# A new written order for 1363 jobs of an attention and two-MoE kernel: the order table, the engine table and one number of the planner

## The chip, the cores and the metric

The kernel runs on one core of one Trainium2 chip. The metric is the device time of one execution in microseconds (us); a version is timed by the median of its runs.

## What is computed

Three stages follow one another, all in FP32. Attention has 2 batches of 8 heads, 768 positions and a head width of 64; each query sees keys less than 16 positions away, and in addition one key for each of the 24 blocks of 32 (the maximum of the block's keys; its value is their mean). The first MoE mixes along the positions, the second convolves along them. Shortened, with shapes as comments:

```python
k_sum = k.reshape(B, H, nb, 32, D).max(axis=3); v_sum = v.reshape(B, H, nb, 32, D).mean(axis=3)
scores_l = where(abs(i - j) < 16, scale * q @ k.T, -1e9)
scores_s = scale * q @ k_sum.T + log(32)
a = softmax(concat([scores_l, scores_s]))            # 768 + 24 columns
x = a @ concat([v, v_sum])                           # then (2, 768, 512)
h = relu(x @ w_in); u, v = h[..., :512], h[..., 512:]
v_s = w_spatial @ layernorm(v) + b_spatial           # 768 x 768 over the positions
x = (u * v_s) @ w_out                                # (2, 768, 512)
h = relu(x @ w_in2)                                  # (2, 768, 1024)
out = (h * sigmoid(conv3(h, conv_w))) @ w_out2       # conv3 over the positions
```

## The kernel before

**Attention.** Two heads of a batch stand together on 128 partitions and are called a pair, n = 0 to 7. A pair has two groups of six blocks of 64 queries; group i is half i mod 2 of pair i div 2, 16 groups in all. For one group TensorE (PE) makes the scores (lines 461, 468 and 474; 96 window keys and 24 block keys for each block), VectorE (DVE) takes the row maximum (478), ScalarE (ACT) does six exps with their sums (482), DVE sums and inverts (485, 488), GpSimd (POOL) or DVE normalises (491). Then PE transposes the weights, three blocks at a time in two parts (495, "first" and "second" transposes), into the one buffer `pt`; each part is copied out by ACT or DVE (517). PE multiplies them with the values (501), and the result is split into a rounded part `xh` (522) and a rest `xl` (523). The scores have two buffers, `s_80` for even groups and `s_81` for odd ones; query and key tiles alternate between even and odd pairs. The block keys come from `keys` (lines 391 to 406), the block means of the values from `means`, on PE (417) for pairs 0 and 2, by a reduction on DVE (424) and a transpose (427) for the others.

**Matrix products.** An FP32 product is three matmuls of rounded parts, high × high, low × high and high × low (lines 309 to 311, 256 or 512 columns each). The weights are split into such parts on ACT, POOL and DVE (`convert`; `sub_lo`, line 278, makes the rest). The first products of MoE 1 are mixed into the attention; then come its mix along the positions, the product of w_out and w_in2, and MoE 2 with its convolution (688), sigmoid (691), gate (694) and output.

**What sets the order.** Nothing is scheduled while the kernel runs. Each piece of work is recorded as a job with the engines that may do it and a planned time, 1363 jobs. `ORDER` names the jobs in the order in which they are issued, two characters each (a number to base 64), and `PICK` names for each job with a choice which of its engines takes it. An engine executes its jobs in this order, each waiting for what it needs. All loads go through SP's one queue in the same order, and a load waits there until its tile is free. The planned times have one effect only: where the plan sees PE idle for 0.5 us or more ahead of the dense products, it puts filler matmuls there, whose result nobody reads (line 740):

```python
if self.fill and gap >= 0.5:
    n = int((gap - 0.1) / 0.22)
    out.append((free.get(e, 0.0), k, e, 0.22 * n, lambda n=n, f=self.fill[1]: f(n)))
```

A load's planned time is its size over `RATE` = 276 KB per us, after which it is taken to land.

Of the kernel before, what the change touches and what calls it, by code (L numbers as in the profile page):

```python
# [20 lines left out]
B, H, S, D = 2, 8, 768, 64  # L21
# [27 lines left out]
STEPV = 4.5  # L49
SIGNS = "ABCDEFGHIJKLMNOPQRSTUVWXYZabcdefghijklmnopqrstuvwxyz0123456789+-"  # L50
ORDER = (
    "AGACAAABADAEAFAgAiASATAjAkAUAVAWAhAXAHAqALBYAYArAsAMBZAIAZAaBbBaBcA3A4A5AbAcAdANBiAJAlAtAuBjBECTCRAOBvAvAwAeBFCUCSA6CVA7"
    "BwA8AKB8DJAmAnBkBlAxAyAzAoBmApBnBGCbBHB9DKA9A0CcBxDIDHDLByBzB0A+A-BAA1A2BRB+BSCoCpB-APCdBdBoBpBBCeCfCgBCBqBrCqDRB1B2BDBe"
    "BfBgAfC1EgEhDSDTCDBhDwCECrCsB3B4DeDfDgBIBKBLAQBsBtChBuBJCWARB5B6C3ETC2CiCjCkEeCXCYCZCaCtCuBMBTBNBOCFBUCGBVCHCIB7EnDUDVBW"
    "CJClCmCvCwCxDrEoDWDXDhCACnCyDiDMCzC0EfE0FNBPBQDjBXDYFODZEpDNDODPDsDxDyDaDkFMEqErEsEiE1DlCBDbDcDdDQDmFPDtDACKEUC5C7C6DnC8"
    "C9EtC+C-CCFBDoDpE2DqCMCLCNCOEuDBDCDDDEDFFVFvFiEjFjE3E4EkDzDuD0D6D7D8D9F8F7DvD1CPD+DGE5CQEvEwD2F9F6D3D4FWFkEEE6EFEGFwD5Gm"
    "EXD-EAEBECFXEYEHFCGDE7EZEaFFEbGQC4FzFGGlElExFYEcEmFZEVFDFHFIFJFaEDGRE8EdF0EyEIE9EJEKELEMGEFQEzGnFKEOEPEQFbERF1F2FLF3F4Gk"
    "GSGTGUF5E+E-FAG6GFGtGuENHHHIFcFdEWGdGeESHRFRFSHSHJGfGgFTGhGiHTFlFmFeF+FfFgGjHUGvGwGxHKFnFoHVHlGGGHHmFpFqHWFhFUGVG7HnHoGI"
    "HLHMFrGJGKG8G9FsHpHbFtHcHdG+FuG-HXGLF-GAHeGMIiGWIDHqFEGBGNJ8J5FyFxGXGYIEH5HfHgGOGPGyGCGZGzIyG0GaHvHwGoHNHOHxHhHiGbGcHjHk"
    "HPHQG1G2GpHyHzH0IzIaLNHAHBIjHYGqGsH6GrHCLUHDINIFHZHaIbH7IcH8H1I3H9G3G4ItG5IIIOHEIJHFISIkH+HrH-HGITIGIULOH2LPIKILH3IAIBH4"  # L60
    "HsICHtHuIuIdIPInIHIlIQIRI9IMIvIVI+IWJbJcJdJeLbI-IeImJvJAIfIgI4IoIXIpI6I5IYIZIqI7I8IrIsIwIxLQLRJBJCJHJRJIJJJKJLJMJwJSJTJU"
    "JVIhJfJgJxJyI0I1KRKvI2JNJOJlJhJWJPJiLWKwJmKxJnJQJzJXJYKHKIKJKKKLJDJEJZKMJoJ9KbKcJjJaKlKdKeKfKgLDKmJ+LEJkKNJFJGJ0JpJqK5LS"
    "J1KOJrJsJ2JtLTKPJuLVJ3KQJ4KhKiLXLYKSK6KjKTKkLdJ-LZLaLcLeLiLfLFKUKVKWKAKBKCLGLHLIK7K8LpKnKoKXLgKyKpM-LJLhLKKYNnMrNAKDKELk"
    "LjLwLlLmMsNBKqKFKGKrLnKsLrKZMtLoKtLqL3K9KaK+K-LALBNJNCNDNKNLLsLtKzLyLuLvNENdNMNNM1M2M3M4K0NeNOLLLxL+KuM5LzL0LMNFNfNgNhMu"
    "MhMvMiMjMkMlMmK1NTMwL1L2L4NGLCL5MFNHL6K2L7K3K4MxL8L9MnMoL-MAMBMCMMNoNUNVOvM6MpM7MqMDMEM8MHMGMTMIMJNPM9M+NQOpO7MKMLO8NiNp"
    "OqNqO1O2MNNIMOMaMPMQNjMRMyOrO3NWNrMzNsNtOsOtMSMUNRO9O4O5M0MVNxNXMWMXMYNuNYO+OwPNPOPTOxPBNZO6PHOuPIMZOyPPPCPJMcMbNkMdMePD"
    "MfMgNSOzNlO-NzJ6NmNyO0N0NvN1PEPFPrPUPVPsN2N3PAN4N6PKN5N7N8PtPQPRPuPwPxNaN9N+NbPSN-OAOBOCPyONPGPePfPgPLODOEPMPhPZQPJ7PjPv"
    "NcPWPzOFP0P2P1NwQCOGPXPaPbP3OIOHOUPiPYOJOKPcQDPdPkPlOLOMQEQFQGQHOOPmPnOPP9QQP+P-OQORPoQmOSQAQBQhPpOTOVP4QnQUOWQVOXOYQIOZ"
    "QJQoQ4PqQWQKQzP5P6QXQYQRQSQTQaQbObOiQ5QLP7RFQMQNQcRGQiQ6QjP8Q0OdQOQ1QpQdQqQrQkQlQsQZRHOaRIQ7RKQ8OcQeRLQtQ2QuQfQ3QvOeOfQw"
    "Q+Q-RJOgQxRARXRcRdRYRMReRfOhRZQ9OjQgRNROOkRBRQOlOmRCQyOnRDRRRSOoR2RuRpSaSbRaRbRgRiRTRERjRkRlSDRqSER3SFSGR4SNSOR5SPRURmRV"  # L70
    "RnRWSHSIRrRsRtRvSJRoSKSLR6SQSRR7R8RPRhRwSSRxRySTScR9R+RzR0SMSdSUSeR-SfR1SpSgSAShSkSVSBSlSiSCSmSWSjTASnSXSxSoSySqTXSzSYSr"
    "S0S1SZS2SsS3S4StS7S5SuS8S6TuS9SvS+SwTIS-TJTBTKTCTLTMTDTNTETOTPTFTSTQT7TTTGTRTUTHTVTfTWTgTYThTZTiTjTaTkTbTlTmTcTpTnTqTdTo"
    "TrTeTsT2TtT3TvT4TwT5UDTxT6UET8UFTyT9UGUHTzUIT+T0UJT1UKT-UNULUAUOUMUPUBUQUCURUSUTUUUXUVUYUWUZUaUbUcUdUeUhUfUiUgUjUkUlUmUn"
    "UoUrUpUsUqUtUuUvUwUxUyU1UzU2U0U3U4U5U6U7U8U-U9VAVBU+VCVDVEVFVGVJVHVKVIVLVMVNVOVPVQVRVS"
)
# [7 lines left out]
class Plan:  # L83
# [118 lines left out]
def block_kernel(ctx, tc, q_in, k_in, vwin, v_in, w_in, w_spT, b_sp, w_outT, w_in2, conv, w_out2, out):  # L202
    nc = tc.nc
    PE, DVE, ACT, POOL, SP = nc.tensor, nc.vector, nc.scalar, nc.gpsimd, nc.sync
# [162 lines left out]
    def load_values(n):
        j, r = n % 2, STEP * NG * n
# [524 lines left out]
```

## Time and profile before

| | before |
|---|---|
| median of 3 runs | 333.48 us (333.2 to 333.6) |
| profiled execution, its own time | 332.87 us |
| span of the profile | 331.1 us |
| PE busy | 326.1 us, 98% of the span |
| DVE, ACT, POOL busy | 234.8, 188.9, 69.4 us |
| share of PE in the chain that ended last | 93% |

The span runs from the first to the last instruction of the profiled execution; the execution's own time has in addition what lies around the span. Busy times are sums over an engine's instructions. PE's weight loads run beside its matmuls and are listed as an engine of their own.

### The profile page before, as it was taken

The numbers are of one execution on the slowest core, as the hardware profiler recorded it, in microseconds if no ns is written. First come the engines' busy times: TensorE is split into PE (matmuls) and PEld (weight loads), VectorE is DVE, ScalarE is ACT, GpSimd is POOL, SyncE is SP. The second block draws the span as 40 slices with busy tenths as digits, with TensorE's granted clock in tenths as the row PEclk, the third lists the DMA queues.
The fourth block names the chain that finished last, engine by engine and source line by source line (L and its number), as shares of the span: only waits on it lengthen the run. The fifth ranks groups of instructions, "written<-read, shape, count | busy, mean of one in ns | idle before, by whom it ended". The sixth has DMA issues, their size and how long they took to land.

```text
span 331.1 us, 6200 instructions
## 1 busy us (share of the span) xinstructions
PE 326.1 (98%) x2391; PEld 269.3 (81%) x2391; DVE 234.8 (71%) x433; ACT 188.9 (57%) x463; POOL 69.4 (21%) x91
## 2 busy tenths in 40 slices
PE   8999999999999999999999999999999999999996
PEld 3677888878888889888988888888888888888886
DVE  5899899876663378678989878898996976470000
ACT  3999888866545443334444355978776865461111
POOL 5696953475040213000111101000000000000000
PEclk9999999999999999999999999999999999999999
DMA  7999649724244300112334423240000010000101
GB/s 220 317 302 318 195 154 319 204 62 122 68 157 157 98 0 0 65 63 90 103 127 129 127 63 127 65 127 1 2 1 1 30 65 32 32 32 34 63 32 65
DMA packets 13325, 34.50 MB, mean 104 GB/s; under 512 B 1648, under 2 KB 3952, under 8 KB 13296
## 3 DMA queue, kind: packets, MB, share of 16 engines
q1 hardware_dynamic: 13296, 34.11, 32.8%
q8 instruction: 19, 0.31, 0.4%
q14 instruction: 10, 0.08, 0.1%
HBM read 30.96 MB, written 3.15 MB: 103 GB/s over the span
## 4 chain that ended last, share of the span: by engine, by line
PE 93%; DMA 3%; ACT 2%; SPq 1%; issue 0%; ACTq 0%
PE late L309 12%; PE late L310 12%; PE late L311 12%; PE mm L309 9%; PE mm L310 9%; PE mm L311 9%; PE xp L501 4%; PE pt L495 3%; PE xp L309 3%; PE xp L310 3%; PE xp L311 3%; PE pt L309 3%; PE pt L310 3%; PE pt L311 3%; DMA a<-vwin 2%; PE s L474 2%
## 5 line engine op out<-in xcount | busy, mean ns | idle before, releaser
L688 DVE SCALAR_TENSOR_TENSOR v<-v,conv_t 128x767 f32<-128x767 f32 x32 | 32.5, 1015 | 9.8 <-ACT v L685 9.5
L482 ACT ACTIVATE a<-s,a 128x120 f32<-128x120 f32 x96 | 33.4, 391 | 0.7 <-DVE a L478 0.6
L278 POOL TENSOR_TENSOR w<-a,w 128x256 fp32r<-128x256 f32 (+1 forms) x15 | 15.2, 1013 | 53.4 <-ACT w L284 52.9
L293 ACT ACTIVATE a<-a 128x512 f32<-128x512 f32 (+1 forms) x25 | 16.3, 650 | 12.4 <-POOL w L278 4.2
L482 ACT ACTIVATION_READ_ACCUMULATOR a<-s,a 128x1 f32 x96 | 22.7, 237 | 0.0
L298 DVE SCALAR_TENSOR_TENSOR a<-a,a 128x512 uint32<-128x512 uint32 (+1 forms) x32 | 19.9, 624 | 3.8 <-ACT a L293 1.4
L491 POOL TENSOR_TENSOR a<-a,a 128x720 f32<-128x720 f32 x15 | 20.8, 1392 | 3.9 <-DVE a L488 3.8
L300 DVE SCALAR_TENSOR_TENSOR a<-a,a 128x512 uint32<-128x512 uint32 (+1 forms) x32 | 19.9, 624 | 0.9
L691 ACT ACTIVATE v<-v 128x768 f32<-128x768 f32 x16 | 13.5, 846 | 9.6 <-DVE v L688 9.6
L309 PE MATMUL late<-xh,a 128*128 128x512 f32 x48 | 18.7, 389 | 0.0
L310 PE MATMUL late<-xl,a 128*128 128x512 f32 x48 | 18.7, 389 | 0.0
L311 PE MATMUL late<-xh,a 128*128 128x512 f32 x48 | 18.7, 389 | 0.0
L694 DVE TENSOR_TENSOR v<-v 128x768 f32<-128x768 f32 x16 | 15.3, 956 | 3.7 <-ACT v L691 3.4
L495 PE MATMUL pt<-ident,a 128*120 128x128 f32 x96 | 16.6, 281 | 0.4 <-ACT a L517 0.4
L729 ACT COPY tmp<-late 128x512 f32<-128x512 f32 x7 | 4.1, 583 | 20.3 <-PE late L311 20.3
L478 DVE TENSOR_REDUCE a<-s 128x6 f32<-128x720 f32 x16 | 14.3, 897 | 1.8 <-PE s L474 1.8
L278 DVE TENSOR_TENSOR a<-tmp,a 128x512 fp32r<-128x512 f32 (+1 forms) x10 | 8.0, 830 | 10.5 <-ACT a L284 10.4
L501 PEld LDWEIGHTS xp<-a,a 120*64 120x64 f32 x384 | 12.5, 137 | 3.4 <-issue 1.9
L685 ACT ACTIVATE v<-v,conv_t 128x768 f32<-128x768 f32 x16 | 15.0, 939 | 0.4
L501 PE MATMUL xp<-a,a 120*64 120x64 f32 x384 | 14.7, 226 | 0.0
L309 PE MATMUL mm<-xh,w 128*128 128x256 f32 (+1 forms) x40 | 14.5, 362 | 0.0
L495 PEld LDWEIGHTS pt<-ident,a 128*120 128x120 f32 x96 | 10.6, 137 | 4.7 <-issue 1.3
(331 smaller groups left out, 1018.4 us busy)
## 6 DMA issues: line engine op xcount, KB each, us to landing
a<-w_in SPq DMA_DIRECT2D x12, 512.0 KB, 3.8
a<-w_out SPq DMA_DIRECT2D x8, 512.0 KB, 3.7
out<-tmp SPq DMA_DIRECT2D x11, 256.0 KB, 2.0
a<-vwin SPq DMA_DIRECT2D x8, 288.0 KB, 6.1
a<-v_in SPq DMA_DIRECT2D x6, 384.0 KB, 6.3
a<-vwin SPq DMA_DIRECT2D x4, 576.0 KB, 7.1
tmp<-w_spT SPq DMA_DIRECT2D x6, 384.0 KB, 3.4
a<-w_in SPq DMA_DIRECT2D x8, 256.0 KB, 5.7
```

The lines of the kernel that those rows point to most:

```text
L278: eng.tensor_tensor(out=lo.r(), in0=src.f(), in1=hi.f(), op=ALU.subtract)
L293: mul = {"ACT": (0.2 + n / 1080, lambda: ACT.mul(fu.f(), half(1).bitcast(F32), 2.0 ** -112)), "POOL": (0.18 + n / 1050, lambda: POOL.tenso ...
L298: add({"DVE": (0.16 + n / 960, lambda: DVE.scalar_tensor_tensor(out=last.u(), in0=fu.u(), scalar=0x80000000, in1=last.u(), op0=ALU.bitwise ...
L300: add({"DVE": (0.16 + n / 960, lambda: DVE.scalar_tensor_tensor(out=fu.u(), in0=fu.u(), scalar=3, in1=last.u(), op0=ALU.logical_shift_left ...
L309: PE.matmul(ps, lhsT=lh, rhs=rh, start=first and i == 0, stop=False)
L310: PE.matmul(ps, lhsT=lh, rhs=rl, start=False, stop=False)
L311: PE.matmul(ps, lhsT=ll, rhs=rh, start=False, stop=last and i == n - 1)
L482: ACT.activation(out=e[:, u, :NK], in_=sv[:, u // GA, u % GA], func=AF.Exp, bias=st[:, 0, u:u + 1], accum_out=sm[:, u, :1])
L491: eng.tensor_tensor(out=e, in0=e, in1=st[:, 1].unsqueeze(2).to_broadcast([128, GB, NK]), op=ALU.mult)
L495: PE.transpose(pt3[:NK, a], e[:, GA * h + a, :NK], ident)
L501: PE.matmul(po[h * D:(h + 1) * D, k * QB:(k + 1) * QB], lhsT=vw3(j)[:NK, g * GB + k, h * D:(h + 1) * D], rhs=pts[:NK, at:at + QB], start=T ...
L688: DVE.scalar_tensor_tensor(out=ct.f()[:, to], in0=hh.f()[:, of], scalar=conv_t[:, 3 * f + k:3 * f + k + 1], in1=ct.f()[:, to], op0=ALU.mul ...
```

## The change

`ORDER` lists the same 1363 jobs in another order; the first 1200 or so of its places differ, and the last 114 of PE's 515 jobs stand as before. `PICK` is new, and with it 49 jobs go to another engine. In `load_kq` the first load of queries gets 166 KB more in its planned size, which moves its planned end back by 0.60 us (166/276), with what that does to the number of fillers; the load itself is as it was. No instruction's data or shape changes. PE has one filler less, 24 after 25.

```diff
 ORDER = (
-    "AGACAAABADAEAFAgAiASATAjAkAUAVAWAhAXAHAqALBYAYArAsAMBZAIAZAaBbBaBcA3A4A5AbAcAdANBiAJAlAtAuBjBECTCRAOBvAvAwAeBFCUCSA6CVA7"
...
+    "AAACABADAEAFAgAiASAGAHATAhAjAkAqAUAVAWALAIA3BYArAXAYAMAsBZAZAaBaBbBcANA4A5AbAcAdAtAuAeAvAJAOBECRBiBjBkBFAlCSCTA6A7CUCVBv"
...
 PICK = (
-    "111101011000010001011110110001000110010111011000011010001010110110000000001000110110011200100011010111011101100001111101"
...
+    "111111211000110001011110110011000110000011010000011010100011111111000010010000110100002100010011001110001100001101001010"
...
         for i in range(qp):
             q0, q1 = S // qp * i, S // qp * (i + 1)
-            dma((q1 - q0) / 2 * 0.84, lambda q0=q0, q1=q1: SP.dma_start(qts[j].ap[:, q0:q1], q_in[b, p][:, q0:q1]), r - 9 + 1.5 * i, writes=[qts[j].tok(q0, q1)])
+            dma((q1 - q0) / 2 * 0.84 + (166 if n + i == 0 else 0), lambda q0=q0, q1=q1: SP.dma_start(qts[j].ap[:, q0:q1], q_in[b, p][:, q0:q1]), r - 9 + 1.5 * i, writes=[qts[j].tok(q0, q1)])
```

Three places of the order, each before and after. The numbers behind the buffers' names count allocations and differ between the two kernels (`a_0_245` of before is `a_0_233`, `a_0_166` is `a_0_157`). The weights of a group lie in `a_0_91`, `a_0_96`, `a_0_97` or `a_0_100` for i mod 4 = 0, 1, 2, 3.

PE before, from the fillers between groups 1 and 2 to the values product of group 2; the rows of the scores ahead of line 474 are left out:

```order
L740 MATMUL mm_84<-ones 128x512
L495 MATMUL pt<-ident,a_0_97 120x128 x3
...
L474 MATMUL s_80<-a_0_95,a_0_245 64x120 x12
L495 MATMUL pt<-ident,a_0_100 120x128 x3
L427 MATMUL xp<-ident,a_0_86 24x128
L309 MATMUL mm_84<-xh_0_93,w_0_164 128x256
L310 MATMUL mm_84<-xl_0_94,w_0_164 128x256
L311 MATMUL mm_84<-xh_0_93,w_0_164 128x256
L495 MATMUL pt<-ident,a_0_100 120x128 x3
...
L474 MATMUL s_81<-a_0_95,a_0_245 64x120 x12
L501 MATMUL xp<-a_0_92,a_0_500 64x64 x12
```

The same stretch after:

```order
L495 MATMUL pt<-ident,a_0_97 120x128 x3
...
L474 MATMUL s_80<-a_0_95,a_0_233 64x120 x12
L427 MATMUL xp<-ident,a_0_86 24x128
L495 MATMUL pt<-ident,a_0_100 120x128 x3
...
L740 MATMUL mm_84<-ones 128x512
...
L474 MATMUL s_81<-a_0_95,a_0_233 64x120 x12
L495 MATMUL pt<-ident,a_0_100 120x128 x3
L501 MATMUL xp<-a_0_92,a_0_519 64x64 x12
```

The two fillers moved from ahead of the second transposes of group 2 to ahead of the scores of group 7 (the second L474). The three 256-column matmuls left the stretch, and the second transposes of group 3 went behind the scores of group 7.

PE before, from the second transposes of group 5 to the first of group 6:

```order
L495 MATMUL pt<-ident,a_0_96 120x128 x3
L309 MATMUL mm_85<-xh_0_93,w_0_164 128x512
L310 MATMUL mm_85<-xl_0_94,w_0_164 128x512
L311 MATMUL mm_85<-xh_0_93,w_0_164 128x512
L495 MATMUL pt<-ident,a_0_97 120x128 x3
```

And after:

```order
L495 MATMUL pt<-ident,a_0_96 120x128 x3
...
L474 MATMUL s_81<-a_0_90,a_0_157 64x120 x12
L495 MATMUL pt<-ident,a_0_97 120x128 x3
L501 MATMUL xp<-a_0_92,a_0_249 64x64 x12
```

The scores of group 9 took the place of three 512-column matmuls, which follow later.

SP before, from a load of keys for pair 3 (`a_0_96`) to one of values; each row is a load, queries of pair 2 go to `a_0_166`, those of pair 3 to `a_0_245`:

```order
L362 DMA a_0_96<-k_in 128x416
L365 DMA a_0_166<-q_in 128x384 x2
L362 DMA a_0_96<-k_in 128x384
L292 DMA a_0_407<-w_in 128x512
L365 DMA a_0_245<-q_in 128x384 x2
L371 DMA a_0_245<-v_in 128x768
```

And after:

```order
L362 DMA a_0_96<-k_in 128x416
L365 DMA a_0_157<-q_in 128x384
L292 DMA a_0_390<-w_in 128x512
L362 DMA a_0_96<-k_in 128x384
L365 DMA a_0_233<-q_in 128x384
L365 DMA a_0_157<-q_in 128x384
L371 DMA a_0_233<-v_in 128x768
L365 DMA a_0_233<-q_in 128x384
```

The second half of pair 2's queries moved from right behind the first half to behind the second half of pair 3's, whose tile the scores of group 3 read until they are done.

## Rows read from the trace of the kernel before

**Rows 1.** By stretch: busy us (instructions) of PE, PEld, DVE, ACT, POOL; granted clock; DMA share.

```profile
0.00:45.00 45.00, 43.04 (x724) 30.67 (x725) 37.48 (x102) 37.18 (x155) 32.47 (x51) 1.00 0.82 253
45.00:250.00 205.00, 205.00 (x1304) 173.19 (x1303) 162.65 (x293) 118.05 (x258) 36.94 (x40) 1.00 0.32 97
```

**Rows 2.** What PE waited for, whole span: total us, times, longest.

```profile
PE mm L740 <- DVE mhalf L734: 1.0, 1, 1.0
PE pt L495 <- ACT a L517: 0.4, 1, 0.4
PE s L474 <- DMA a<-q_in: 0.4, 1, 0.4
```

**Rows 3.** Timeline of PE, 19 to 27 us: start, duration, instructions, idle before.

```profile
19.41 0.79 PE L474 MATMUL s<-a,a 64*64 64x120 f32 x24
20.12 0.54 PE L495 MATMUL pt<-ident,a 128*120 128x128 f32 x3
20.59 0.92 PE L501 MATMUL xp<-a,a 120*64 120x64 f32 x24
21.45 0.60 PE L740 MATMUL mm<-ones 128*128 128x512 bf16 x2
21.90 0.54 PE L495 MATMUL pt<-ident,a 128*120 128x128 f32 x3
22.38 0.23 PE L461 MATMUL s<-a,ones 64*64 64x72 bf16 x4
...
23.27 0.54 PE L495 MATMUL pt<-ident,a 128*120 128x128 f32 x3
...
24.00 0.29 PE L311 MATMUL mm<-xh,w 128*128 128x256 f32 x1
24.72 0.54 PE L495 MATMUL pt<-ident,a 128*120 128x128 f32 x3 [0.44 <-ACT a L517]
...
26.09 0.92 PE L501 MATMUL xp<-a,a 120*64 120x64 f32 x24
```

**Rows 4.** Timeline of PE, 33.5 to 45 us.

```profile
33.80 0.55 PE L495 MATMUL pt<-ident,a 128*120 128x128 f32 x3
34.10 0.47 PE L309 MATMUL mm<-xh,w 128*128 128x512 f32 x1
34.41 0.39 PE L310 MATMUL mm<-xl,w 128*128 128x512 f32 x1
34.64 0.40 PE L311 MATMUL mm<-xh,w 128*128 128x512 f32 x1
35.00 0.52 PE L495 MATMUL pt<-ident,a 128*120 128x128 f32 x3
...
41.26 0.40 PE L311 MATMUL mm<-xh,w 128*128 128x512 f32 x1
41.67 0.52 PE L495 MATMUL pt<-ident,a 128*120 128x128 f32 x3
```

**Rows 5.** Timeline of ACT, 21 to 25 us.

```profile
21.34 0.51 ACT L517 COPY a<-pt 120x384 f32<-120x384 f32 x1
...
24.01 0.29 ACT L482 ACTIVATION_READ_ACCUMULATOR a<-s,a 128x1 f32 x1
24.10 0.57 ACT L517 COPY a<-pt 120x384 f32<-120x384 f32 x1
```

**Rows 6.** Timeline of SP's queue, 9 to 20 us: two issues of queries.

```profile
12.98 1.49 SPq L365 DMA_DIRECT2D a<-q_in  x2
```

**Rows 7.** Transfers issued from 14.1 to 14.2 us: times, KB, us to landing.

```profile
a<-q_in SPq DMA_DIRECT2D x1, 192.0 KB, 4.9
```

**Rows 8.** The chain that ended last, one piece: start, duration.

```profile
7.75 6.85 DMA a<-vwin
```

**Rows 9.** Timeline of DVE, 250 to 253 us.

```profile
250.59 1.95 DVE L278 TENSOR_TENSOR a<-v,a 128x768 fp32r<-128x768 f32 x2
```

**Rows 10.** Timeline of PE, 253 to 255 us.

```profile
254.13 0.39 PE L309 MATMUL late<-a,a 128*128 128x512 f32 x1
```

More of the change, by code (lines that the diff above doesn't have):

```diff
@@ L51 @@
 ORDER = (
-    "AGACAAABADAEAFAgAiASATAjAkAUAVAWAhAXAHAqALBYAYArAsAMBZAIAZAaBbBaBcA3A4A5AbAcAdANBiAJAlAtAuBjBECTCRAOBvAvAwAeBFCUCSA6CVA7"
-    "BwA8AKB8DJAmAnBkBlAxAyAzAoBmApBnBGCbBHB9DKA9A0CcBxDIDHDLByBzB0A+A-BAA1A2BRB+BSCoCpB-APCdBdBoBpBBCeCfCgBCBqBrCqDRB1B2BDBe"
-    "BfBgAfC1EgEhDSDTCDBhDwCECrCsB3B4DeDfDgBIBKBLAQBsBtChBuBJCWARB5B6C3ETC2CiCjCkEeCXCYCZCaCtCuBMBTBNBOCFBUCGBVCHCIB7EnDUDVBW"
-    "CJClCmCvCwCxDrEoDWDXDhCACnCyDiDMCzC0EfE0FNBPBQDjBXDYFODZEpDNDODPDsDxDyDaDkFMEqErEsEiE1DlCBDbDcDdDQDmFPDtDACKEUC5C7C6DnC8"
@@ L56 @@
[L56 to L71, printed above, removed]
+    "AAACABADAEAFAgAiASAGAHATAhAjAkAqAUAVAWALAIA3BYArAXAYAMAsBZAZAaBaBbBcANA4A5AbAcAdAtAuAeAvAJAOBECRBiBjBkBFAlCSCTA6A7CUCVBv"
@@ new lines @@
+    "BwBxAwAxAKAmBlBmAnAyB8BGCbA8AzAoA9DJA0BnCcApBKB9DKDLB-ByBzB0DHBLDIA+A-BABHCoBoA1A2CpCdAPBdBBBpBqBCBDBrCeB+DRBeCqB1B2CfAf"
+    "DeBfBgC1BREeDSCDCECgB3B4AQBsChCrCsEgBhBSEhDTDfDgCtBICWBJCXBtCiBuCjCkCYARB5ETB6BTBUBVCZBMBNBOC2EnBWCFCuCGCHCvB7DUDVCICBCK"
+    "CAC5DADwEfDWBPBQCaClCwCxE0BXCJEoDhCmFNDXDYCnCyEpDMDiDZDxCzC0DaDrC3DNDODsDjDkFMDyDlDPDbEUDQFBCCFODcDmDnDtEqErEsEVC6FPE1E2"
+    "EiDdC7C8C9C+EtEuDoDpDqC-CLFVCME3E4CNCOCPFiDzD0DuFjDvFCFvJ5EvEwEWEXFWFQD6FkD7D8D9DBD1FDF7E5D2D3DCCQDDDEF6DFD4E6D+EEEFEjF8"
@@ new lines @@
+    "GmEYD5D-EGEAEBDGECEHF9FXGDGQEZFYGnC4EaEbEkE7ElExE8EmFFFGGlEIEOEcEDEJEKFHFIFJFKEdGRGSFZFzEyE9GkEPELFwGdGEGFEMENEzEQE+FEF0"
+    "FLG6GtERHHFaFbGeF1F2F3GTESGfGgGhF4F5GGGHFxGiGjFcHRHIHSHTHJHUHVGuE-FlGUFAFdHKFeFmHLFnG7HlFRFSFTHWGoHXGvGIGVFoHbHmHnFfFgFU"
+    "HoHpHcHdFpHMFqG8F+FhGwH5HeFrGJGKFsItGLHfHqHvHNHOHgGxHYG9HhH6GMGWFtFuGyHPGXHwHxF-H7GYGAGBGCH8GNHyIiHZHaGOGPHiGZGzG+G-G0Ga"
+    "GbH9GcIjHQIDG1IyGpGqGrIuG2FyHAIzIIIEIkHjHzGsHkHBG3INHCH0H1IOIPH+H-G4HDG5HEH2IFIvIaIbIAHrHsHFHGIdIeIfIgIBH3IcI3HtIlIQISIT"
@@ new lines @@
+    "ICH4IXI0IGIwI1IUIRIHI9I+HuI4InIYIoIJIKILIMIhImI-JAJHJIIVIWJJJlJRJKIZIqIrIpI6I7LNIsI8JLJMI5JBIxLOJmJSJTJUJnJbJcJdKbJeJ9Jo"
+    "JCJDJEJVJWJNJXJOJFJGJpLPLQLRJfJgJPJQJhJiJYJ+J-JvJ8LULbKAJwJxJyKRKSJzJ0K5J1LDJZJaJqJ2KlLWI2KHKIKJKvLSLTKBKCKDKELVLiLEJjLX"
+    "LYJ3K6JrJkKFJsKcKwLFKxKyLdKmLZLaKKLcLpKdKLLGKMKNKnKeKfJtJ4KOLeLfJuKTKgK7K8KhKiKGLgKjKPLhLHLkKkLjLlLILJKUM-KoKVKWNALmLnLr"
+    "KpLwKqKzK0K9KXLoNBK+LqKrL3KYLsLKKZKaLtKsLuLvLxNJNKLyLzL0L+L5KtNCL1KQK1M1L2LLNDKuMhMiMjK-LAL4MkL6MlMmNLLBLCMnK2NMNENNNnM2"
@@ new lines @@
+    "K3NONTL7M3M4L8M5NdNeM6NfM7NoNUNVK4NWMFNpNgM8L9L-M9MoMpMAMMO1LMNFMBMCM+MDMHOpNhOqMEMGNGNHMrMsMtMuMvNqMwNiOrMINrMJMONsMxMK"
+    "MLMNMqNPMPMQOvOsPBO2O7O3O8O9OwOxNQNRMRMyNIOtMzNXNjOyPNNtPTNYMSO+PUO4MTMUOuMVMWMaPOMXMYMcMZPVMbNkNSMdNlMeMfM0NZPHO-PAOzMg"
+    "NxNyNzO5O0N0N1N2PWPXN4O6N6N3PZPPPCPQPRPeNuPDNmPfN5N7PSN8NaN9PEPIN+PYJ6N-J7OBPJOAOCODPgPaPKPFPLPhPiPbPcOEOFQUPMOGOHPdPwPx"
+    "PkPrPyPzOIOJOKOLP0P1NvPlPmQCQDPnQEOMPGONOPPsOOOUNbObOQOROSOTPoNcQFPtPuPvQGP9P+P-QAQzQ0QPQVQWQXP2P3QBQIQJQKPjQ4OWP4PpOVOX"
@@ L72 @@
+    "OYQLP5P6QMOZQHP7OdQNQZQ1PqQQQRQSQTOaOcQ2Q3QmQ5Q6P8QnQOQYOeOfQoQhQ7QiQ8Q+QaQ9Q-RAOgOhQjQkQpQqQlQsQbQcQtQuRBQvRCQwQdQeRFSN"
+    "OiOjQxRcRXRYOkOlRdReQfOmQyQgRDRZRKOnRLRaRuNwRMRpRNSORGRqROOoRERHRIRJRQRRRbRfRgQrRSRiRjRkSDSERTRUSFSGRlRmRVSaRnR2RrRsRtRv"
+    "SPSQSHR3SIR4RWSJRoSKSLRPRhR5R6RwSSSRR7R8RxRySTSbScR9R+RzR0SMSdSUSeR-SfR1SpSgSAShSkSVSBSlSiSCSmSWSjTASnSXSxSoSySqTXSzSYSr"
     "S0S1SZS2SsS3S4StS7S5SuS8S6TuS9SvS+SwTIS-TJTBTKTCTLTMTDTNTETOTPTFTSTQT7TTTGTRTUTHTVTfTWTgTYThTZTiTjTaTkTbTlTmTcTpTnTqTdTo"
@@ L76 @@
 PICK = (
-    "111101011000010001011110110001000110010111011000011010001010110110000000001000110110011200100011010111011101100001111101"
-    "100100010001111002100010010010001000001100110010000000000000000000000000200000000200200200200"
+    "111111211000110001011110110011000110000011010000011010100011111111000010010000110100002100010011001110001100001101001010"
+    "100001000000101112100010000010011000000000101000000000000000000000000200200000000200200200200"
 )
```

## The prediction

> **What bounds the kernel now.** I read the stretches first [rows 1]. From 45 to 250 us TensorE (PE) is busy for the whole 205.00 us, and what follows is the same dense work to its last matmul. The granted clock is 1.00 in both. So PE is the bound, and what a new order can win lies in the first 45 us, where PE is busy 43.04 us. The list of what PE waits for [rows 2] shows three waits of 0.1 us or more: for the constant in front of the first filler, for the first queries, and 0.4 us for a copy on ScalarE (ACT). No order of the same loads brings the first two forward: in both orders the first queries are the fourth load on SP's queue, behind the same two halves of keys and the same part of w_in.
>
> A list of waits is not enough, since short stalls fall under its limit. Therefore I read PE's timeline by pitch, from one start to the next [rows 3, 4]. The third 256-column matmul starts at 24.00, the three transposes (L495) behind it at 24.72: a pitch of 0.72 us, where 256 columns take 0.12 (half the 0.23 us between 34.41 and 34.64 for 512 columns). That is a stall of **0.60 us**: the transposes write the one buffer `pt`, and the copy that empties it (L517) starts on ACT only at 24.10, right behind the exps of group 5 [rows 5]. The same happens twice more, smaller: from 34.64 to 35.00, 0.36 against 0.23, so **0.13 us**, and from 41.26 to 41.67, 0.41 against 0.23, so **0.18 us**. In sum 0.91 us. I found no other stall of this kind before 70 us, and later the feeders of PE run ahead by more.
>
> **The change, part by part.** The work on PE is the same, one filler fewer. When the order on PE changes, its end moves by three things only: idle time, fillers in the path, and extra cost where neighbours differ.
>
> *The three stalls.* In the new order the second transposes of group 3 stand behind the scores of group 7, and between the second transposes of group 5 and the first of group 6 stand the scores of group 9 instead of three 512-column matmuls. The scores take 0.89 us (22.38 to 23.27) [rows 3], more than a copy of 0.51 to 0.57 [rows 5]. These two stalls go: **−0.73 us**. The third stays. Between the second transposes of group 7 and the first of group 8 the same three 512-column matmuls stand in both orders (the last of them at 41.26) [rows 4], and the copy is ACT's in both: 0, with −0.18 as the bound if the copy starts sooner, and +0.4 if it queues behind work that ACT newly gets there.
>
> *What takes the place of the first.* Up to 21.45 the two orders end alike. Before, two fillers bridge the time until the copy at 21.34 is done (21.34 + 0.51 = 21.85) [rows 5], and L495 follows at 21.90. In the new order the fillers are gone from there, PE idles these 0.45 us, and L495 starts at 21.90 all the same: nothing won. The scores of group 6 follow, to 23.27, then L427 and the first transposes of group 3. Their predecessor's copy is in both orders one that VectorE makes; it now stands behind one more operation there, which I take as 0.07 us. So they start at 23.34 and are through at 23.34 + 0.48 = 23.82 (0.48 is 21.90 to 22.38). Next come the scores of group 7. They write the same score buffer that the exps of group 5 read, and those end at 24.01 + 0.29 = 24.30 [rows 5]. Before, the scores of group 7 came at about 25.2 and that end did not matter. Now it does: a wait of 24.33 − 23.82 = 0.51, filled by the two fillers (0.45), so that they cost nothing extra. Then group 7 takes 0.89 to 25.22, the transposes 0.48, and the values product (L501) that started at 26.09 starts at 25.70. This looks like 0.39 won, but three 256-column matmuls (the last at 24.00; three times 0.12, about 0.4 with the start) are still owed and come later. The stall of 0.60 is therefore paid back as 0.51 + 0.07: **+0.58 us**.
>
> *The second.* Its place gets work that has to be done anyway. Nothing is paid back that I can see.
>
> *Switches of tiling.* PE changes between 64-row work (scores), 120×64 work (L501) and full tiles (everything else). From transposes to L501 the pitch is 20.12 to 20.59, 0.47 us [rows 3]. From transposes to a full 512-column matmul it is 0.30 (33.80 to 34.10), and that first matmul takes 0.31 where the second takes 0.23 [rows 4]. So the transposes themselves cost 0.30 + 0.08 = 0.38 among full tiles, and the switch 0.47 − 0.38 = 0.09 us. Counted over the whole order there are 52 switches before and 54 now: **+0.18 us**. The bounds are 0 (hidden by the weight load) and 0.4 us (twice the price at each).
>
> The Trainium skill, page "TensorEngine Tiling (Array Packing)", section "Key Properties", states "Mode switching requires drain". By this rule a search that trades stalls for switches can lose what it wins; it gives no price, and the trace's 0.09 us agrees with it. Without that rule the sum would be 0.18 us lower.
>
> *Loads.* The change to `load_kq` alters only a number in the planner. The order of SP's queue changes. The second values load for pair 0 keeps the same bytes ahead of it. Most other loads are within one place of where they were, and cost nothing as long as PE's next job is late for another reason. One is not, see rival B.
>
> *Engine choices.* 49 jobs move between ACT, VectorE and GpSimd. Two go to ACT between the exps of groups 5 and 7 (a copy of 0.51 and a cast); the exps behind come about 0.4 us later and find PE busy with other work. VectorE takes over some sub_lo jobs of the weight conversions before 205 us. The tightest late place that I found is at 254 us: two subtractions on VectorE end at 250.59 + 1.95 = 252.54, the matmul that needs the second starts at 254.13 [rows 9, 10], so 1.59 us are free, and the gate work leading there starts earlier in the new order. I take 0, and 0 to 0.5 us for the range.
>
> **Sum.** −0.73 + 0.58 + 0.18 = +0.03 us. The profiled execution took 332.87 us; its span of 331.1 lies 1.8 below that, and nothing in that part changes. 332.87 + 0.03 = 332.90. The median of the runs is 333.48, 0.61 above the profiled execution, so I expect a median of 332.90 + 0.61 = **333.5 us**. About 0.2% (0.67 us) is what this measurement can tell from no change: faster begins under 332.8, slower above 334.15.
>
> **Rivals.**
> A, faster: the wait in front of group 7 does not come about, because the exps of group 5 end earlier or the fillers cover it from a later start, and nothing is paid back. Then −0.73 + 0.18 = −0.55, **332.9 us**; with free switches, or with the third stall gone as well, 332.75, just past the bound. For it: ACT's choices in this stretch change. Against: the exps follow one another on ACT with copies alone between them [rows 5].
>
> B, slower, by one load: the second half of pair 2's queries. Before, it was issued right behind the first half; in the new order it stands behind pair 3's second half, which waits for the scores of group 3 to leave the tile. Before, this waiting load was the second of the two at 12.98, and ended its issue at 14.47 [rows 6]; the moved one would then be issued at about 14.55. By the row for a query load issued just there (4.9 us) [rows 7] it lands at 19.45, when group 5's scores start their matmuls on it (19.41) [rows 3]: no loss, and 0.45 us of the idle time ahead of 21.90 would absorb more. By the slowest row of this stretch (a load of `vwin`, 6.85 us) [rows 8] it lands at 21.40, 1.99 late; less 0.45 this costs 1.54, and the median is 333.5 + 1.5 = **335.0 us**. It decides (0.65 us) from a landing after about 20.5.
>
> C, slower, by the clock: if PE's granted clock falls from 2.4 to 1.2 GHz in a new gap, matmuls take twice their time for a while; ten 512-column matmuls more at 0.23 us each are 2.3 us, **335.8 us**. The rows speak against it: 1.00 in both stretches [rows 1], with gaps of 0.60 us and the wait for the queries in them, and the new gaps are no longer. The Trainium skill, page "TensorE: Matmul & The Clock Gate", section "What's actually happening", names idleness as what throttles; the trace has no fall to show it.
>
> D, the change does nothing that can be measured: this is my forecast: what it wins it pays back within 3 us.
>
> **Numbers.** Forecast with D 0.55 (332.9 to 334.1), A 0.22 (0.14 of it under 332.8), B 0.10, C 0.03; 0.10 for further stalls of some tenths each, from engine moves that I took as 0, to the slower side. So faster 0.14, same 0.63, slower 0.23. Range: below, A with free switches and the third stall gone gives −0.91, 332.57, and I take 332.6; above, 0.5 for engine moves, 0.22 more for switches (0.4 in all) and 0.4 at the third stall give 333.5 + 1.1 = 334.6, which takes in part of B.
>
> **What would show it.** Right: no stall in front of the transposes at the first two places, and one of about 0.2 us left at the third; two fillers in front of group 7's scores, these starting at about 24.3 with the exps of group 5 just over; an idle 0.4 us before 21.9; the values product of pair 2 at 25.7; the same pitches from 70 us on. Wrong: group 7's scores at 23.8 (A); a wait of group 5's scores for a query load (B); a granted clock below 1.00 after the start (C); PE idle between 70 and 254 us.

## The result, and the profile after

The changed kernel took 335.48 us (median of 7 runs) beside 333.22 us for the kernel before: ratio 1.0071, 95% interval 1.0047 to 1.0094. It is slower by 2.3 us, and outside the range of the prediction. (The ratios here and below leave out runs in a slow state, and are not the quotients of the medians beside them.) Its profiled execution took 336.23 us with a span of 334.4 us, 3.3 us more than before. Nearly all of the difference arises in the first 45 us: the 256-column matmul that starts at 44.66 before starts at 47.94 here, 3.28 us later, and the last matmul of all is 3.36 us later.

The same two stretches as in [rows 1], in the profile of the changed kernel (busy us of PE, PEld, DVE, ACT, POOL with instructions; then granted clock, DMA share, GB/s):

```profile
0.00:45.00 45.00, 40.44 (x629) 28.27 (x630) 35.50 (x97) 35.09 (x140) 30.39 (x49) 1.00 0.92 269
45.00:250.00 205.00, 205.00 (x1381) 173.49 (x1382) 160.38 (x299) 118.67 (x272) 35.74 (x39) 1.00 0.30 94
```

PE idles 45 − 40.44 = 4.56 us in the first stretch, where it idled 45 − 43.04 = 1.96; the dense stretch is full again, at the same clock. The list of PE's waits, beside [rows 2], says what for (us in total, times, longest):

```profile
PE xp L501 <- ACT a L517: 1.6, 1, 1.6
PE s L474 <- DMA a<-q_in: 1.3, 1, 1.3
PE mm L740 <- DVE mhalf L734: 1.0, 1, 1.0
PE pt L495 <- ACT a L517: 0.3, 1, 0.3
PE s L461 <- ACT a L482: 0.2, 1, 0.2
```

Two are new and large, 2.9 us together. They stand in PE's timeline here:

```profile
1.04 5.73 PE L740 MATMUL mm<-ones 128*128 128x512 bf16 x13 [1.04 <-DVE mhalf L734]
6.69 0.27 PE L461 MATMUL s<-a,ones 64*64 64x72 bf16 x4
...
7.00 0.81 PE L474 MATMUL s<-a,a 64*64 64x120 f32 x24
...
22.03 0.54 PE L495 MATMUL pt<-ident,a 128*120 128x128 f32 x3 [0.33 <-ACT a L517]
...
24.48 0.23 PE L461 MATMUL s<-a,ones 64*64 64x72 bf16 x4
...
25.38 0.54 PE L495 MATMUL pt<-ident,a 128*120 128x128 f32 x3
27.57 0.92 PE L501 MATMUL xp<-a,a 120*64 120x64 f32 x24 [1.65 <-ACT a L517]
...
34.60 0.84 PE L474 MATMUL s<-a,a 64*64 64x120 f32 x24 [1.28 <-DMA a<-q_in]
...
44.58 0.40 PE L311 MATMUL mm<-xh,w 128*128 128x512 f32 x1
44.94 0.51 PE L495 MATMUL pt<-ident,a 128*120 128x128 f32 x3
```

At 27.57 the values product of group 2 (pair 1; the prediction's last paragraph names it pair 2's) starts 1.65 us late. The copy on ACT that the row names is one that this product does not read, and it ends at 27.12 + 0.46 = 27.58, after the product has begun (timeline of ACT):

```profile
26.78 0.43 ACT L293 ACTIVATE a<-a 128x256 f32<-128x256 f32 x1 [1.13 <-DMA a<-w_in]
27.12 0.46 ACT L517 COPY a<-pt 120x384 f32<-120x384 f32 x1
```

What the product needs is the load of `vwin` for pair 1. SP's queue shows its issue (the first of four from 18.48), and the list of transfers issued in that moment how long it took (times, KB, us to landing):

```profile
11.50 0.33 SPq L362 DMA_DIRECT2D a<-k_in  x1
14.41 1.65 SPq L365 DMA_DIRECT2D a<-q_in  x2
...
18.48 4.04 SPq L375 DMA_DIRECT2D a<-vwin  x4
```

```profile
a<-vwin SPq DMA_DIRECT2D x1, 288.0 KB, 9.0
```

It landed at 18.48 + 9.0, about 27.4. Before, the same load was issued later, at 19.72 (the first of three), and landed earlier, at 25.1:

```profile
19.72 2.63 SPq L375 DMA_DIRECT2D a<-vwin  x3
```

```profile
a<-vwin SPq DMA_DIRECT2D x1, 288.0 KB, 5.4
```

The queries of pair 4 follow the same pattern: issued at 23.80, landed at 34.5 (10.7 us), where before it was 23.34 and 31.75 (8.4 us):

```profile
a<-q_in SPq DMA_DIRECT2D x1, 384.0 KB, 10.7
```

```profile
a<-q_in SPq DMA_DIRECT2D x1, 384.0 KB, 8.4
```

The queue above shows where the time was lost. SP issues nothing from 11.50 + 0.33 = 11.83 to 14.41. The load at its head is the second half of pair 3's queries, which may not overwrite its tile until the scores of group 3 are done (PE, 13.55 + 0.79 = 14.34). In the kernel before this load waits as well, until 14.15. But three loads of 640 KB together (a part of w_in, pair 2's second and pair 3's first half of queries) stand ahead of it there and behind it here; the other way went one load of 256 KB. From 10 to 20 us the transfers moved this much, first the changed kernel, then the kernel before:

```profile
DMA packets 1613, 2.70 MB, mean 270 GB/s; under 512 B 185, under 2 KB 1226, under 8 KB 1612
```

```profile
DMA packets 1908, 3.34 MB, mean 334 GB/s; under 512 B 221, under 2 KB 1298, under 8 KB 1906
```

0.64 MB are missing, 1.9 us at 334 GB/s. The transfers thin out only after SP has stood still for a while: from 16 to 18 us the DMA share is 0.75 in the changed kernel (the first row) and 1.06 before (the last three figures are granted clock, DMA share and GB/s):

```profile
16.00:18.00 2.00, 2.00 (x41) 1.38 (x39) 1.54 (x5) 2.00 (x11) 1.71 (x3) 1.00 0.75 237
16.00:18.00 2.00, 2.00 (x42) 1.44 (x42) 1.55 (x5) 1.60 (x10) 1.65 (x3) 1.00 1.06 394
```

The two loads that PE waits for land 2.4 and 2.7 us later than before, a little more than these 1.9 us.

The start lost a little, too. The second half of pair 0's keys is third on the queue now, was first, and VectorE gets it only at 5.67 (rows of VectorE in the changed kernel):

```profile
5.67 0.56 DVE L397 TENSOR_REDUCE a<-a 128x12 f32<-128x384 f32 x1 [1.47 <-DMA a<-k_in]
6.26 0.31 DVE L403 TENSOR_SCALAR a<-a 128x288 f32<-128x288 f32 x1
```

So the last operation on these keys ends at 6.57 (before 5.05 + 0.31, about 5.37), and the scores' matmuls on the queries start at 7.00 (before 6.73). In this execution PE did not wait for the keys, though: the 13 fillers ahead of the first scores run until 6.69 (the first rows of PE above). They take 5.73 us here and took 5.03 before (the last section says why):

```profile
1.04 5.03 PE L740 MATMUL mm<-ones 128*128 128x512 bf16 x13 [1.04 <-DVE mhalf L734]
6.00 0.23 PE L461 MATMUL s<-a,ones 64*64 64x72 bf16 x4
...
6.73 0.84 PE L474 MATMUL s<-a,a 64*64 64x120 f32 x24 [0.38 <-DMA a<-q_in]
```

Those 0.70 us and the 2.60 us of idle time more are the 3.3 us of the span.

### The profile page after: what moved, and what is told of

Same layout as the page of the kernel before. It is cut to its first block, busy times and chain, and to the rows that moved or that the text cites. A ratio compares the mean times of both kernels' runs of the same rounds, so it can differ in the third digit from the quotient of the medians.

```text
span 334.4 us, 6183 instructions
## 1 busy us (share of the span) xinstructions
PE 326.8 (98%) x2390; PEld 270.0 (81%) x2390; DVE 233.3 (70%) x437; ACT 189.3 (57%) x463; POOL 66.1 (20%) x87
## 3 DMA queue, kind: packets, MB, share of 16 engines
q1 hardware_dynamic: 13296, 34.11, 33.1%
## 4 chain that ended last, share of the span: by engine, by line
PE 91%; DMA 5%; ACT 1%; SPq 1%; issue 0%; DVE 0%; POOL 0%; ACTq 0%; POOLq 0%
PE late L309 12%; PE late L310 12%; PE late L311 12%; PE mm L309 9%; PE mm L310 9%; PE mm L311 9%; DMA a<-q_in 3%; PE xp L310 3%; PE xp L309 3%; PE xp L311 3%; PE xp L501 3%; PE pt L310 3%; PE pt L309 3%; PE pt L311 3%; PE pt L495 2%; PE s L474 2%
## 5 line engine op out<-in xcount | busy, mean ns | idle before, releaser
L278 POOL TENSOR_TENSOR w<-a,w 128x256 fp32r<-128x256 f32 (+1 forms) x12 | 11.7, 983 | 64.5 <-ACT w L284 64.3
L482 ACT ACTIVATION_READ_ACCUMULATOR a<-s,a 128x1 f32 x96 | 21.6, 225 | 0.0
L309 PE MATMUL late<-xh,a 128*128 128x512 f32 x48 | 18.7, 389 | 0.0
L310 PE MATMUL late<-xl,a 128*128 128x512 f32 x48 | 18.7, 389 | 0.0
L311 PE MATMUL late<-xh,a 128*128 128x512 f32 x48 | 18.7, 389 | 0.0
L517 ACT COPY a<-pt 120x384 f32<-120x384 f32 x23 | 11.1, 484 | 9.0 <-PE pt L495 8.9
```

The lines of the kernel that those rows point to most:

```text
L309: PE.matmul(ps, lhsT=lh, rhs=rh, start=first and i == 0, stop=False)
L310: PE.matmul(ps, lhsT=lh, rhs=rl, start=False, stop=False)
L311: PE.matmul(ps, lhsT=ll, rhs=rh, start=False, stop=last and i == n - 1)
L482: ACT.activation(out=e[:, u, :NK], in_=sv[:, u // GA, u % GA], func=AF.Exp, bias=st[:, 0, u:u + 1], accum_out=sm[:, u, :1])
```

## The experiments

Two theories stood against each other. **L (loads)**: SP's queue, blocked from 11.83 to 14.41, makes both new waits. **E (engine choices)**: the wait at 27.57 comes from ACT, where a multiplication for w_in newly stands in the queue and ACT idles 1.13 us for those weights at 26.78; the other wait comes from the order of bytes on the queue. The time varied from run to run by a microsecond and more on the chips of the experiments, so each ratio is taken to the kernel before, run between them.

**e1_query_later**: the blocked load goes behind three others (SP's order of the changed kernel, − and +):

```diff
 L362 DMA a_0_96<-k_in 128x384
-L365 DMA a_0_233<-q_in 128x384
 L365 DMA a_0_157<-q_in 128x384
 L371 DMA a_0_233<-v_in 128x768
-L365 DMA a_0_233<-q_in 128x384
+L365 DMA a_0_233<-q_in 128x384 x2
```

> The changed kernel with one load moved three places back on SP's queue: the second half of pair 3's queries, which waits for group 3's scores, now stands behind the second half of pair 2's queries, the values of pair 1 and the first half of pair 3's queries. Theory L (loads): in the changed kernel SP stands still from 11.83 to 14.41 us behind this load, the transfer engines run dry, and everything later lands some 2 us late; that makes both new waits of PE (1.65 us at 27.57, 1.28 us at 34.60). It expects the vwin of pair 1 to land before 26 us, both waits gone or under 0.4 us in sum, and 335.5 - 2.7 = 332.8 us (332.5 to 333.3). Theory E (engine choices): the wait at 27.57 comes from ScalarE, which now has a multiplication for w_in in its queue and idles 1.13 us for those weights, and the wait at 34.60 from the order of bytes on the queue; it expects at most 0.5 us of gain, 335 us.

Measured: 333.52 us, ratio 0.9995 (0.9978 to 1.0011). One load moved by three places takes the loss back. The largest waits of PE in its profile:

```profile
PE mm L740 <- DVE mhalf L734: 1.0, 1, 1.0
PE s L474 <- POOL a L403: 0.6, 1, 0.6
```

Both large waits are gone. From 10 to 20 us it moved 3.49 MB, the `vwin` of pair 1 landed at 23.2 and the queries of pair 4 at 29.1. The 0.6 us are a wait of group 2's scores for keys in this run. The time itself lies 0.2 us above the range of theory L (332.5 to 333.3), which was reckoned from 333.22 us for the kernel before; that kernel took 333.86 us beside this run.

**e2_before_blocked**: the hole alone, put into the kernel before.

```diff
 L362 DMA a_0_96<-k_in 128x384
-L292 DMA a_0_407<-w_in 128x512
-L365 DMA a_0_245<-q_in 128x384 x2
+L365 DMA a_0_245<-q_in 128x384
+L292 DMA a_0_408<-w_in 128x512
+L365 DMA a_0_245<-q_in 128x384
 L371 DMA a_0_245<-v_in 128x768
```

> The kernel before with one load moved two places forward on SP's queue: the second half of pair 3's queries stands right behind the keys of pair 3, ahead of a part of w_in and the first half of pair 3's queries. Theory L: SP stands still from about 11.8 to 14.2 us here too, some 2 us of transfers are lost, the vwin of pair 1 lands near 27 us in place of 25.1 (needed at 26.1) and the queries of pair 4 near 34 in place of 31.75 (needed at 32.2): waits of PE of 1.2 and 0.5 us, 333.2 + 1.7 = 334.9 us (334.3 to 335.5). Theory E: no change, 333.2 us.

Measured: 334.61 us, ratio 1.0037 (1.0010 to 1.0064). Its queue and the wait that follows:

```profile
10.92 0.42 SPq L362 DMA_DIRECT2D a<-k_in  x1
14.14 0.33 SPq L365 DMA_DIRECT2D a<-q_in  x1
```

```profile
27.48 0.92 PE L501 MATMUL xp<-a,a 120*64 120x64 f32 x24 [1.53 <-DMA a<-vwin]
```

With all compute engines in the order of before, SP stands still from 11.34 to 14.14, and the values product waits 1.53 us for `vwin`. The size is near the 1.2 us expected, and the last matmul of all is 1.5 us later than in the profile of the kernel before; the second wait did not come, since group 8's scores were late by then anyway (the queries landed at 33.1, their matmuls start at 33.61). Theory E, which expected no change, fails here.

**e3_mul_on_gpsimd**: the multiplication goes back to GpSimd (one digit of `PICK`, job 132).

```diff
-    "111111211000110001011110110011000110000011010000...
+    "111111211000110001011110110011000110000111010000...
```

> The changed kernel with one engine choice put back: the multiplication for the first part of w_in's third row block goes to GpSimd again instead of ScalarE. Theory L: ScalarE no longer idles for these weights, but the values product still waits for the vwin of pair 1 (landing at 27.4): PE's wait at 27.57 stays within 0.2 us of 1.65, and the time at 335.5 us. Theory E: that wait goes, 335.5 - 1.6 = 333.9 us.

Measured: 334.79 us (5 runs), ratio 1.0036 (1.0019 to 1.0054); this is 0.7 us under what theory L said, but within the scatter of the changed kernel itself (1.0038 in after_again). The trace decides. The three views are transfers issued at 18.96 (to landing), PE, PE:

```profile
a<-vwin SPq DMA_DIRECT2D x1, 288.0 KB, 7.9
```

```profile
26.99 0.92 PE L501 MATMUL xp<-a,a 120*64 120x64 f32 x24 [0.65 <-ACT a L517]
...
33.51 0.90 PE L474 MATMUL s<-a,a 64*64 64x120 f32 x24 [0.74 <-DMA a<-q_in]
```

The product starts just behind the landing (18.96 + 7.9 = 26.9), as in the changed kernel (27.57 after 27.4), though ACT no longer stands still for these weights. In all four profiles that have this wait the product starts 0.13 or 0.14 us after the landing of `vwin` (the changed kernel, after_again, e2 and this run). The waits are shorter because this run lost 0.5 us more at the start, where the keys came at 6.39: PE asks later for loads that come when they come. The number expected for that wait (within 0.2 of 1.65) was missed for this reason.

**e4_loads_of_before**: the changed kernel with the first 34 loads in the order of before, at the hole's place for instance (buffers are numbered anew):

```diff
 L362 DMA a_0_96<-k_in 128x384
-L365 DMA a_0_233<-q_in 128x384
-L365 DMA a_0_157<-q_in 128x384
+L292 DMA a_0_244<-w_in 128x512
+L365 DMA a_0_117<-q_in 128x384 x2
```

> The changed kernel, its order on all compute engines and its fillers as they are, with the first 34 loads in the order of the kernel before. Theory L: both waits go, and the start of the first scores comes back by 0.3 us, since the second half of the keys lands earlier again: 335.5 - 2.9 - 0.2 = 332.4 to 333.3 us. What is left against the kernel before is then what the prediction summed up (+0.03 us). Theory E: the wait at 27.57 stays, since ScalarE's order is that of the changed kernel: 334 to 335 us.

Measured: 335.83 us (4 runs), ratio 1.0060 (1.0039 to 1.0080). Both theories missed. There is no hole (3.23 MB from 10 to 20 us, `vwin` landed at 25.7), but another queue blocks (timelines of POOL and PE):

```profile
24.95 0.42 POOL L294 TENSOR_SCALAR a<-a 128x256 f32<-128x256 f32 x1 [2.58 <-DMA a<-w_in]
...
26.05 0.85 PE L474 MATMUL s<-a,a 64*64 64x120 f32 x24 [0.76 <-POOL a L389]
```

In the changed kernel GpSimd takes the weights of one half of a row block at 21.87. In the old order of loads these are issued at 19.89 and land at 24.9; GpSimd idles 2.58 us for them, and behind it wait the keys for group 7's scores. PE has further waits of 0.6 and 0.5 us behind it that the changed kernel has not. An order of loads fits the order of the engines that consume them, and here swapping one alone cost about as much as the hole.

**e5_one_place** and **after_again**: the blocked load one place later only, and the changed kernel itself beside it.

```diff
 L362 DMA a_0_96<-k_in 128x384
+L365 DMA a_0_157<-q_in 128x384
 L365 DMA a_0_233<-q_in 128x384
-L365 DMA a_0_157<-q_in 128x384
```

> The changed kernel with the blocked load (second half of pair 3's queries) only one place later, behind the second half of pair 2's queries. A dose of theory L: one load of 192 KB more is under way while SP stands still, worth about 0.65 us of transfers at 300 KB per us; the hole shrinks by as much and the two waits of 2.9 us in sum by 0.6 to 0.9, so 0.5 to 1.0 us under the changed kernel run beside it, and still 1 us or more over the kernel before. Theory E: no change against the changed kernel.

> The changed kernel once more, on the same chip as the three others, as their base. Theory L: 1.5 to 2.3 us over the kernel before, with PE's waits for vwin and for the queries of pair 4 again 2.5 to 3 us in sum, less what the start already lost.

Measured: e5_one_place 334.41 us, ratio 1.0029 (1.0004 to 1.0053); after_again 334.80 us, ratio 1.0038 (1.0017 to 1.0060). The step of 0.4 us is in the expected direction and a little under the 0.5 to 1.0 expected, and the intervals overlap: by the times alone it is not resolved. The loss of e5_one_place against the kernel before is 0.8 us, where 1 or more was expected; that of the changed kernel is 1.2 us here, where it was 2.3 at first and 1.5 to 2.3 was expected, and its two waits are 2.2 us in sum, expected 2.5 to 3. In the traces the dose shows: 3.11 MB from 10 to 20 us against 2.75, and `vwin` at 25.4 against 27.1. The largest waits of after_again:

```profile
PE xp L501 <- DMA a<-vwin: 1.5, 1, 1.5
PE mm L740 <- DVE mhalf L734: 1.0, 1, 1.0
PE s L474 <- DMA a<-q_in: 0.7, 1, 0.7
```

The same two, and here the profile names the load itself. The profiled run of e5_one_place has neither, but waited 1.1 us at the start for the keys. It took 333.64 us, 0.8 less than the median of its runs, so what the median run lost is not shown.

**e6_start_too** (run twice): as e1, and the first eight loads as before, with the changed kernel's fillers (the first rows, buffers numbered anew).

```diff
+L362 DMA a_0_91<-k_in 128x384
 L362 DMA a_0_91<-k_in 128x416
-L292 DMA a_0_154<-w_in 128x512
-L362 DMA a_0_91<-k_in 128x384
-L365 DMA a_0_157<-q_in 128x384
+L292 DMA a_0_109<-w_in 128x512
+L365 DMA a_0_111<-q_in 128x384
```

> The blocked load three places later, and the first eight loads in the order of the kernel before (second half of pair 0's keys first), with the changed kernel's fillers. Theory L with the start: in the changed kernel the second half of these keys comes third and lands at 5.3 to 6.4 us instead of 3.2, so that the last operation on the keys ends 0.9 to 1.9 us later and, in most runs, after the first queries have landed; putting it first takes back 0.2 to 0.6 us of the 333.52 us of the run with the load alone moved: 333.0 to 333.4 us, ratio to the kernel before 0.998 to 0.9995. If the start were set by the queries alone: no change against that run.

> The kernel of e6_start_too once more beside e8_cast_behind, as its base: 0.998 to 1.000 of the kernel before, 0.2 to 0.5 us over e8_cast_behind if the two moves behind it are worth what the traces show.

Measured: 333.12 us, ratio 0.9987 (0.9970 to 1.0003), and 333.78 us, ratio 0.9996 (0.9980 to 1.0012). The keys are ready at 5.4 and 5.5 in the two profiles instead of 6.2 to 7.3, and the queries (landed at 6.7 in both) are again what the first scores wait for. Since the queries come late too in these runs, little is won: the ratios stand at e1's or 0.1% under it, and the gain is not resolved.

**e7_no_payback**: as e6, and three 256-column matmuls in place of the two fillers ahead of group 7's scores (PE's order):

```diff
 L495 MATMUL pt<-ident,a_0_100 120x128 x3
-L740 MATMUL mm_84<-ones 128x512
-L740 MATMUL mm_84<-ones 128x512
+L309 MATMUL mm_84<-xh_0_93,w_0_227 128x256
+L310 MATMUL mm_84<-xl_0_94,w_0_227 128x256
+L311 MATMUL mm_84<-xh_0_93,w_0_227 128x256
```

> As e6_start_too, and the three 256-column matmuls moved ahead of group 7's scores in place of the two fillers there, which are left out. By the prediction's working the wait for the exps of group 5 is 0.51 us, filled by fillers; work that has to be done anyway (0.36 to 0.44 us) fills it as well. Expected 0.35 to 0.45 us under e6_start_too: 332.6 to 333.0 us, ratio to the kernel before 0.997 to 0.9985. If group 7's scores waited for something else that comes later, no gain.

Measured: 333.32 us, ratio 0.9994 (0.9975 to 1.0012); no gain. In the trace the matmuls do fit into the wait, and something else happens later:

```profile
24.41 0.23 PE L461 MATMUL s<-a,ones 64*64 64x72 bf16 x4
...
31.35 0.37 PE L474 MATMUL s<-a,a 64*64 64x120 f32 x8
32.17 0.64 PE L474 MATMUL s<-a,a 64*64 64x120 f32 x16 [0.45 <-issue]
```

Group 7's scores start at 24.41, as in e6_start_too, so in this trace the matmuls ahead of them cost nothing. But PE then stands still for 0.45 us in the middle of group 8's scores, between two matmuls that need nothing new; the profile names no releaser ("issue"), and I could not settle what it was.

**e8_cast_behind**: as e7, and on ACT a cast of weights goes behind the relu that frees an accumulator bank.

```diff
 L584 ACTIVATE v_0_1035<-mm_84 128x256
+L584 ACTIVATE v_0_1035<-mm_85 128x512
 L284 CAST w_0_798<-a_0_109 128x512
-L584 ACTIVATE v_0_1035<-mm_85 128x512
```

> As e7_no_payback, and on ScalarE one cast of weights behind the relu that frees PE's second accumulator bank instead of ahead of it. In the traces of after_again and e6_start_too PE waits for that relu near 61 and 58 us (0.2 to 0.6 us). If this wait was real: gone, and with the 0.35 us that the moved matmuls won in the trace of e7_no_payback a time of 0.3 to 0.6 us under the kernel before, ratio 0.998 to 0.9992. If the time is set by the landing of loads in each run instead, the ratio stays within 0.9985 and 1.0005 and no gain can be told.

Measured: 333.13 us, ratio 0.9981 (0.9963 to 1.0000), and 0.65 us under e6_repeat beside it, though the two intervals overlap. This version is clearly better than the changed one, and better than the kernel before by about 0.6 us at the edge of what these runs can tell. Why is not shown. PE's wait for that relu is not in its list, but neither is it in those of e6_repeat, of e7_no_payback and of the changed kernel's first profile; and the profiled executions of e8_cast_behind and e6_repeat took 333.35 and 333.26 us, so their traces don't show the gain.

What the profiles show together (MB moved from 10 to 20 us; landing in us; PE's waits for the two loads):

| kernel | MB | `vwin` pair 1 | queries pair 4 | waits | ratio to before |
|---|---|---|---|---|---|
| before | 3.34 | 25.1 | 31.75 | 0 | 1 |
| after | 2.70 | 27.4 | 34.5 | 1.65 + 1.28 | 1.0071 |
| after_again | 2.75 | 27.1 | 33.5 | 1.49 + 0.69 | 1.0038 |
| e3 | 2.71 | 26.9 | 33.4 | 0.65 + 0.74 | 1.0036 |
| e2 | 2.92 | 27.3 | 33.1 | 1.53 + 0 | 1.0037 |
| e5 | 3.11 | 25.4 | 31.5 | 0 | 1.0029 |
| e4 | 3.23 | 25.7 | 31.9 | 0 | 1.0060 |
| e6 | 3.33 | 23.8 | 28.7 | 0 | 0.9987 |
| e1 | 3.49 | 23.2 | 29.1 | 0 | 0.9995 |

The profile columns are of one execution each, the ratio of all runs; e4 loses by waits of another kind.

## Why the prediction was wrong, point by point

**The step that failed** is *Loads*: "Most other loads are within one place of where they were, and cost nothing as long as PE's next job is late for another reason." The sum has no term for loads; they measured 1.65 + 1.28 = 2.9 us of waits in the profile. I compared places and bytes ahead, and both were right: 25 of the first 34 loads are within one place, and fewer bytes stand ahead of the `vwin` of pair 1 than before. But a queue in order also stops. A load that waits for its tile holds all loads behind it, and if too few are under way the transfers run dry. Rival B had the right place and the right wait (14.41 as the issue, from the scores of group 3), and priced it for one load only, the one directly behind. That one was harmless, as worked out: pair 2's second half landed at 18.7 and group 5's scores did not wait. The loads seven and twelve places behind the blocked one, with 1.0 and 0.5 us of margin in the kernel before (25.1 for 26.09, 31.75 for the matmuls on these queries at 32.23), were the ones to look at. e1 takes the hole away and the loss goes; e2 puts the hole into the kernel before and the wait comes.

The Trainium skill, page "DMA: Bandwidth & Descriptors", section "Anatomy of one DMA — SWDGE (gpsimd) path", says where such a wait stands: "any semaphore wait happens on the issuing sequencer before dispatch". The section describes another way of issuing, but the trace agrees for SP's queue: nothing issued from 11.83 to 14.41.

**What bounds the kernel**: right that PE is the bound from 45 us on. Wrong was that the first queries decide the start in either order. "Behind the same two halves of keys" counted bytes, and not that the keys need two more operations after they land; those now end at 6.57, behind the queries, which land at 6.15 (before 6.59). In the profiles of after_again, e5_one_place and e3 PE waits for them, 0.2, 1.1 and 1.5 us. In the first profile of the changed kernel the fillers end later still (6.69), and the 0.27 us by which the scores' matmuls are late there come from them.

**The three stalls**: right. The first two are gone; the third stays, at 44.58 to 44.94, 0.36 − 0.23 = 0.13 us.

**What takes the place of the first**: right to within 0.05 us. The scores of group 7 start at 24.48, right after the exps of group 5 end (the next operation on ACT starts at 24.22, its last sum ends at 24.43); 24.33 was forecast and the stretch runs 0.12 us late (22.50 after 22.38). In e6_start_too, without the late loads, the values product of pair 1 starts at 25.78; forecast 25.70, the stretch 0.06 late. The trace of e7 shows the payback from the other side: work put into that wait does not move the scores behind it.

**Switches of tiling**: the two that were added can't be seen by themselves in any run here. At the matmul that stands at 44.66 before, e6_start_too is 0.05 us early (44.61) after scores of group 3 that were 0.13 late (13.24 for 13.11): 0.18 won in between, where the sum said 0.03 lost. So the three terms together were right to about 0.2 us.

**Engine choices**: the multiplication on ACT that I passed over did make ACT idle for 1.13 us, without effect on PE (e3). A relu behind a cast on ACT, which I took as 0, holds PE up near 60 us in some executions only: from the first of three 256-column matmuls to the 512-column one that needs the relu it is 0.44 us in the changed kernel's first profile, in e6_repeat and in e7, 0.62 in e6_start_too and 0.92 in after_again. So it is no part of the 2.3 us as they were profiled.

**Rivals**: A did not come about. C neither, as a fall in a new gap: the granted clock is 1.00 from 7.05 us on, and the product behind the longest new gap takes 0.92 us at 27.57 as it did at 26.09 before. The forecast fell by a mechanism next to B with a price that B lacked.

## What to carry to other kernels

When an order of loads changes, don't only compare places and bytes: find each load that has to wait for its tile, see when it is released, and count what is under way behind the last one issued. If that runs out sooner, the loads behind are late, and the price is paid at the load with the least margin, which here stood seven and twelve places on. e4 shows the same for GpSimd's queue, where an operation waits for its weights and holds up the keys behind it.

## What the runs showed of the hardware that was not expected

The pace of the first transfers varies from run to run of one and the same order: the second half of pair 0's keys, third on the queue, landed at 5.3 us in e1, 5.65 in the changed kernel and 6.4 in e3; as first load it landed at 3.1 to 3.2 in all seven profiles that have it there. That the scatter of the times comes from there is likely but not shown: the changed kernel lost 2.3 us in one comparison and 1.2 in another.

The first fillers run at two paces, and where the pace changes differs between executions. From start to start a filler of 512 columns takes 0.43 us (which is 1.2 columns per ns) at first and 0.22 us later, and the faster pace comes between about 3.9 and 5.7 us in nine of the twelve profiles, but not before the fillers end in those of the changed kernel, e4 and e8. The first scores start at 6.69 or 6.70 us in these three, at 5.3 to 6.2 in the others. The views list the granted clock as 1.00 for this stretch too; but the trace's first record of it (1.00) begins only at 7.05 us in the changed kernel. In the kernel before it begins at 5.22 and in e3 at 4.29, and there the fillers turn faster at the same times. So the slow fillers ran at the lower level, 1.2 GHz, and the changed kernel was profiled in an execution where that lasted long.

PE can stand still without a releaser: 0.45 us within group 8's scores in e7_no_payback.
